# Keys and queries of six units turned by the vector engine instead of by matmul, in a delta-rule and mixer kernel

## The chip, the cores and the metric

One core of a Trainium2 chip runs the whole program. The metric is the time on the device in microseconds (us); the median of five runs is compared. The engines have short names in what follows: PE (matrix engine), DVE (vector), ACT (scalar), POOL (GpSimd), SP (the engine that here does nothing but issue DMAs).

## What is computed

```python
k_n = k / (np.linalg.norm(k, axis=-1, keepdims=True) + 1e-06)
for t in range(S):
    y[:, :, t] = einsum('bhd,bhde->bhe', q[:, :, t], state)
    v_old = einsum('bhde,bhd->bhe', state, k_n[:, :, t])
    state = state + beta_t * einsum('bhd,bhe->bhde', k_n[:, :, t], v[:, :, t] - v_old)
x = y with the heads side by side            # (4, 768, 384)
u = x + (xt @ U @ V).transpose(0, 2, 1)      # xt = x.transpose(0, 2, 1)
out = u + np.maximum(u @ w_ch1, 0.0) @ w_ch2
```

There are 4 batches, 8 heads, 768 tokens and 48 numbers per head. The mixer has rank 32 for the tokens and 1536 hidden channels. All data are 32-bit floats on the chip.

## The kernel before

The recurrence is cut into chunks of 64 tokens (`L`), 12 per batch. Half a batch, six chunks of all eight heads, is a *unit*; units 0 to 7 are numbered through the batches, so batch b has units 2b and 2b+1. For each unit the kernel prepares what does not depend on the state: the products of keys with keys (`pg`) and of queries with keys (`qk`), and the inverse of a triangular 64x64 matrix per chunk and head (`zt`).

- `load_keys(n)`, `load(n)`, `load_queries(n)` fetch k, v and q with tokens on partitions (`kn`, `vn`, `qn`), eight DMAs each. From unit 2 on all are issued by SP.
- `norms(n)` squares and sums the keys (the squares are put into a buffer that is not yet in use), and makes the factors `cp` and the scaled v.
- `grams(n)` has key pairs and query pairs of chunks. For each, `turn` brings two chunks onto head-dimension-on-partitions with four PE transposes (L529) and one ACT copy (L535) into `kq`; then `products` multiplies (L553) and the results go to `pg` (ACT) or, masked, to `qk` (DVE, L569).
- `blocks(n)` sends `pg` through DRAM into 96 rows of 32x32 blocks (L624, L635), scales them (`gs`, L652), inverts them on DVE with 31 pairs of operations (L668, L674), sends the result through DRAM again (L683) and reads it back in two layouts (`zt` L707, `zc` L710); two groups of small matmuls (`p_x` L722, `p_v` L736) fill the off-diagonal quarter. 32x32 blocks of `zc` are turned by DVE (`turned`, L695).
- `recur(b)` walks through the 12 chunks of a batch. Each chunk is a chain PE (`p_y`, L870), DVE (`rhs`, L900), PE (`p_s`, L907), ACT (`z`, L916), PE (L921, L929), DVE (`s`, L944).
- `front(b, i)` is the low-rank part of the mixer and the turning of its result; `wide(b, i)` has the two large matmuls, `p_f` (L1038) and `p_o` (L1058), in groups of three matmuls, and the stores of the result (L1029).

The weights arrive as two 32-bit words per number and are converted by DVE slice by slice (`load_weights`).

The order of all instructions is decided when the program is built. The parts above are Python generators; a planner in `run` keeps a modelled clock per engine, knows which named events (`need`, `emitted`) a part waits for, and emits at each step the part that could start earliest, with a preference for parts of a lower place number. Costs such as `step(sp=2.6)` are the planner's guesses. On the chip every engine then works through its own instructions strictly in that order, and waits at semaphores.

Buffers matter for the change: `kq`, `pg`, `qk` and `vn` have two copies, so those of unit n come free when `rec(n-2)`, the recurrence over unit n-2, is done; `qn` has one copy, used in turn by all units but unit 1.

Of the kernel before, what the change touches and what calls it, by code (L numbers as in the profile page):

```python
# [9 lines left out]
FP32 = mybir.dt.float32  # L10
# [17 lines left out]
def kernel(  # L28
# [154 lines left out]

    ident = const.tile([128, 128], FP32, name="ident")
    make_identity(nc, ident)
    beta_sb = unit.tile([B * H, S], FP32, name="beta_sb", tag="kq")
    nc.gpsimd.dma_start(out=beta_sb, in_=beta.rearrange("b h s -> (b h) s"))
    upper = conv.tile([128, 128], FP32, name="upper", tag="wide")
    nc.gpsimd.memset(upper, 1.0)
# [92 lines left out]
    def load_weights():  # L282

        slices = list(weight_slices())
        loaded = {}

        def start(i):  # L290
            dst, src, groups = slices[i]
            n = dst.shape[1]
            if i % 2:
                wide = stage[:, 0 : 2 * n].bitcast(I32).rearrange("p (n two) -> p n two", two=2)
            else:
                wide = conv.tile([128, n, 2], I32, name="wide")
# [12 lines left out]

        def load_all():  # L310
            for i in range(len(slices)):
                yield need(("weights", i - 2), *[("v", 0)] * (i == 1), *[("opened", 1)] * (i == 2))
                yield from start(i)

        begin(load_all(), 2.03)
        for i in range(len(slices)):
            dst = slices[i][0]
            yield need(("landed", i))

            if dst.shape[1] == WIDE and i >= 2 + KT * DFF // WIDE:  # L320
                yield need(("ksq", 2), *[("keys turned", 2, c) for c in range(UC // 2)])
# [38 lines left out]
            emitted(("weights", i), 0.2)  # L360
# [55 lines left out]
    def load(n):  # L416

        yield need(("rec", n - 2))
        kq = unit.tile([128, UC, 2, 2, 2 * L], FP32, name="kq")
        pg = unit.tile([128, UC, 2, 2, L], FP32, name="pg")  # L420
        qk = unit.tile([128, UC, 2, 2, L], FP32, name="qk")
        made[n] = kq, pg, qk
# [16 lines left out]
    def load_queries(n):  # L439
        yield need(("turned", n - 1), ("turned", 0))  # L440
        yield from fetch(n, "q", qn[:, :, :, 0:D], q, (0, 0))

    def norms(n):

# [6 lines left out]
        kn = keys[n][:, :, :, 0:D]  # L451
        if n > 2:

            ksq = made[n][0][:, UC // 2 :].rearrange("p c j i t -> p (c j i t)")
# [61 lines left out]
    def grams(n, place):  # L516


        yield need(("k", n), ("room", n), ("pg", 0 if n == 1 else -1))
        kn = keys[n]  # L520
        kq, pg, qk = made[n]

        def turn(ts, places):
# [8 lines left out]
                        ident,  # L532
                    )
            yield step(act=0.6, then=0.1, give=("one",))
            nc.scalar.copy(places, p_t)  # L535

        def products(c0, i):

# [8 lines left out]
            for c in range(2):  # L547
                for j in range(2):
                    for par, x in QUADS:
                        rows, cols = half(par, D), half(x)  # L550

                        to = half(1 - x) if par == 1 and i == 0 else cols
                        nc.tensor.matmul(  # L553
                            p_g[par][to, c, j],
                            kq[rows, c0 + c, j, 0, cols],
                            kq[rows, c0 + c, j, i, cols],
                            start=True,
                            stop=True,
                        )
# [14 lines left out]
                    )  # L574

        def key_pair(c0):
            if n > 2 and c0 + 2 > UC // 2:
                yield need(("ksq", n))
            yield from turn([(kn, c0), (kn, c0 + 1)], kq[:, c0 : c0 + 2, :, 0])
            emitted(("keys turned", n, c0 // 2))  # L580
            yield from products(c0, 0)
            emitted(("p", n, c0 // 2), 0.5)

        def query_pair(c0):
            yield need(("q", n), ("p", n, c0 // 2))
            yield from turn([(qt, c0), (qt, c0 + 1)], kq[:, c0 : c0 + 2, :, 1])
            yield from products(c0, 1)
            emitted(("g", n, c0 // 2), 0.5)

# [8 lines left out]
        yield need(*[("g", n, i) for i in range(UC // 2)])  # L598
        emitted(("grams", n))
        emitted(("turned", n))  # L600

    def blocks(n):

# [262 lines left out]
    def recur(b):  # L866
        def from_state(p, kq, cu, i, s_old, first):

            for j, par, x in heads:
                nc.tensor.matmul(  # L870
                    p[half(x ^ par), par, D * (2 * i + j) : D * (2 * i + j) + D],
                    kq[half(par, D), cu, j, i, half(x)],
                    s_old[half(par, D), x, j],
                    start=first and j == 0,
                    stop=(i == 0),
# [202 lines left out]
    order += [(recur(b), 5 + 0.01 * b) for b in range(1, B)]  # L1078
    for n in range(2, 2 * B):
        at = 0.01 * n + (3 if n < 4 else 5)  # L1080
        order += [(load_keys(n), at + 0.1), (load(n), at + 0.1), (load_queries(n), at + 0.5)]
        order += [(norms(n), at + 0.2), (grams(n, (at + 0.3, at + 0.4)), at + 0.3)]
        order.append((blocks(n), at + 0.6 if n == 2 else 5.6 + 0.01 * n))
    for b in range(B):
# [36 lines left out]
```

## Time and profile before

| | us |
|---|---|
| median of 5 runs (lowest, highest) | 677.28 (674.7, 681.59) |
| the profiled execution | 677.28 |
| its span from first to last instruction | 675.5 |
| PE busy in the span | 622.2 |
| DVE busy in the span | 318.1 |
| ACT busy in the span | 199.1 |

The span falls into these parts, by the start of the instructions on PE: units 0 and 1 are prepared up to about 59 us; `recur(0)` runs from 59 to 130; `front(0)` follows, and the mixer's first large matmul starts at 151.5. `recur(1)` runs from 196.5 to 290, `recur(2)` from 320.7 to 415 and `recur(3)` from 453 to 542, each with the mixer of the batch before it in its gaps. From 550 us on only the mixer is left. The granted clock of PE was 0.50 between 31 and 120 us and 1.00 from 151 us on.

In the tables of the profile that follow, a line names the source line, the engine, the operation and the tiles it writes and reads; `x8` is a count, and what stands in brackets is how long the engine had been idle before the instruction and what ended the wait. `SPq` is SP issuing DMAs: its duration is the issuing, not the transfer.

### The profile page before, as it was taken

To read this page: it belongs to the slowest core of one execution; us is meant where nothing else is said; L and a number is where in the kernel's file an instruction comes from. 1 tells how busy PE (TensorE), PEld (TensorE's weight loads), DVE (VectorE), ACT (ScalarE), POOL (GpSimd) and SP (SyncE) were. 2 spreads that over 40 slices of the span, in tenths; PEclk is the share of its full clock that TensorE was granted. 3 is DMA by queue.
4 is the path that set the end of the run, shared out by engine and by line. 5 is a ranking of instruction groups with operands and counts; after the bars stand their busy time and mean duration, and the time that the engine had idled before them with its cause. 6 is when DMAs were issued, how large, how long until landed. Compare 5 with 4: busy or idle time off the path is not lost.

```text
span 675.5 us, 19682 instructions
## 1 busy us (share of the span) xinstructions
PE 622.2 (92%) x8676; PEld 400.3 (59%) x8676; DVE 318.1 (47%) x795; ACT 199.1 (29%) x487; POOL 43.3 (6%) x84
## 2 busy tenths in 40 slices
PE   5649898759999999989999999999999999999997
PEld 4438787526555566546556655665555555555554
DVE  6667687579888124872942287368111011000000
ACT  2406455524221362144314422323221221110210
POOL 6451000100100000000000000000000000000000
PEclk9955555859999999999999999999999999999999
DMA  8586736552711332246033312410300000000000
GB/s 123 117 209 143 157 104 186 139 112 40 196 39 37 71 65 60 49 100 116 14 69 71 78 38 54 72 55 2 60 14 26 1 1 24 12 1 23 13 11 24
DMA packets 143892, 46.00 MB, mean 68 GB/s; under 512 B 136960, under 2 KB 140032, under 8 KB 143808
## 3 DMA queue, kind: packets, MB, share of 16 engines
q1 hardware_dynamic: 133952, 30.99, 22.6%
q0 software_dynamic: 3552, 12.88, 6.6%
q10 hardware_dynamic: 6304, 0.89, 0.8%
q8 instruction: 68, 1.11, 0.7%
q14 instruction: 16, 0.13, 0.1%
HBM read 33.62 MB, written 11.11 MB: 66 GB/s over the span
## 4 chain that ended last, share of the span: by engine, by line
PE 81%; DVE 7%; DMA 6%; ACT 2%; SPq 2%; issue 1%; ACTq 1%; DVEq 0%
PE p_o L1058 28%; PE p_f L1038 27%; PE p_y L870 4%; PE p_g L553 3%; PE p_t L529 3%; PE p_s L907 2%; PE p_s L921 2%; DMA scr<-xt 2%; PE p_y L929 2%; DVE xt L674 2%; DVE prod L668 2%; PE p_u L1005 1%; PE p_e L794 1%; DMA scr<-pg 1%; PE p_h L995 1%
## 5 line engine op out<-in xcount | busy, mean ns | idle before, releaser
L1038 PE MATMUL p_f<-ut,w_sb 128*128 128x384 f32 x576 | 202.3, 496 | 0.2 <-ACT h_f L1023 0.2
L1058 PE MATMUL p_o<-w_sb,h_f 128*128 128x384 f32 x576 | 201.1, 495 | 0.0
L1038 PEld LDWEIGHTS p_f<-ut,w_sb 128*128 128x128 f32 x576 | 104.5, 190 | 63.8 <-issue 0.6
L1058 PEld LDWEIGHTS p_o<-w_sb,h_f 128*128 128x128 f32 x576 | 104.8, 190 | 63.2
L1023 ACT ACTIVATE h_f<-p_f 128x384 f32<-128x384 f32 x96 | 47.1, 490 | 202.9 <-PE p_f L1038 202.8
L1028 DVE TENSOR_TENSOR x<-x,p_o 128x384 f32<-128x384 f32 x24 | 13.2, 553 | 131.5 <-PE p_o L1058 131.5
L674 DVE TENSOR_TENSOR xt<-xt,prod 96x112 f32<-96x112 f32 (+21 forms) x216 | 70.4, 326 | 7.4
L668 DVE TENSOR_TENSOR prod<-gs,xt 96x112 f32<-96x112 f32 (+21 forms) x216 | 70.0, 324 | 6.4 <-ACT xt L641 0.3
L553 PE MATMUL p_g<-kq 48*64 48x64 f32 x1536 | 39.8, 251 | 8.9 <-DVE qk L569 7.7
L944 DVE TENSOR_TENSOR s<-s,p_s 128x192 f32<-128x192 f32 x40 | 14.1, 352 | 69.9 <-PE p_s L921 66.3
L553 PEld LDWEIGHTS p_g<-kq 48*64 48x64 f32 x1536 | 33.5, 160 | 17.8 <-DVE qk L569 7.2
L951 ACT COPY x<-p_y 64x192 f32<-64x192 f32 x96 | 30.0, 313 | 39.2 <-PE p_y L929 34.0
L870 PEld LDWEIGHTS p_y<-s,kq 48*64 48x64 f32 x1408 | 29.0, 151 | 19.9 <-issue 11.2
L535 ACT COPY kq<-p_t 128x512 f32<-128x512 f32 x48 | 27.4, 587 | 40.2 <-PE p_t L529 40.0
L916 ACT COPY z<-p_s 128x192 f32<-128x192 f32 x48 | 15.3, 318 | 74.8 <-PE p_s L907 74.5
L870 PE MATMUL p_y<-s,kq 48*64 48x48 f32 x1408 | 34.8, 240 | 0.8 <-DVE s L944 0.6
L900 DVE TENSOR_TENSOR rhs<-vn,p_y 128x192 f32<-128x192 f32 x44 | 15.5, 352 | 41.5 <-PE p_y L870 41.0
L907 PEld LDWEIGHTS p_s<-rhs,zt 64*64 64x64 f32 x704 | 16.7, 149 | 22.4 <-issue 17.8
L921 PEld LDWEIGHTS p_s<-z,kn 64*64 64x64 f32 x704 | 16.1, 151 | 19.3 <-issue 16.5
L907 PE MATMUL p_s<-rhs,zt 64*64 64x48 f32 x704 | 22.4, 244 | 3.7 <-DVE qk L569 1.7
L637 POOL MEMSET xt<- 96x1056 f32 x6 | 5.9, 978 | 276.3 <-DMA scr<-xt 276.3
L529 PE MATMUL p_t<-ident,kn 128*128 128x128 f32 x84 | 16.3, 332 | 7.7 <-DMA kn<-in_k_dram 7.0
(122 smaller groups left out, 525.0 us busy)
## 6 DMA issues: line engine op xcount, KB each, us to landing
wide<-in_moe_w_ch_dram POOLq DMA_DIRECT2D x6, 768.0 KB, 5.7
stage<-in_moe_w_ch_dram POOLq DMA_DIRECT2D x6, 768.0 KB, 5.9
out_dram<-x SPq DMA_DIRECT2D x24, 192.0 KB, 1.9
kn<-in_k_dram SPq DMA_DIRECT2D x60, 72.0 KB, 2.8
qn<-in_q_dram SPq DMA_DIRECT2D x48, 72.0 KB, 3.2
vn<-in_v_dram SPq DMA_DIRECT2D x48, 72.0 KB, 2.5
gs<-scr SPq DMA_DIRECT2D x8, 384.0 KB, 3.7
scr<-xt SPq DMA_DIRECT2D x8, 384.0 KB, 4.3
```

The lines of the kernel that those rows point to most:

```text
L529: nc.tensor.transpose(p_t[:, x, j], t[:, c, 2 * j : 2 * j + 2].rearrange("p s d -> p (s d)"), ident,)
L535: nc.scalar.copy(places, p_t)
L553: nc.tensor.matmul(p_g[par][to, c, j], kq[rows, c0 + c, j, 0, cols], kq[rows, c0 + c, j, i, cols], start=True, stop=True,)
L668: nc.vector.tensor_tensor(out=prod, in0=gb[:, :, j : j + 1, j + 1 :].to_broadcast([NP, split, m, w]), in1=xb[:, :, 0:m, j : j + 1].to_broa ...
L674: nc.vector.tensor_tensor(out=xb[:, :, 0:m, j + 1 :], in0=xb[:, :, 0:m, j + 1 :], in1=prod, op=ALU.subtract,)
L870: nc.tensor.matmul(p[half(x ^ par), par, D * (2 * i + j) : D * (2 * i + j) + D], kq[half(par, D), cu, j, i, half(x)], s_old[half(par, D), ...
L907: nc.tensor.matmul(p_s[half(x), par, D * (2 + j) : D * (2 + j) + D], zt[half(x ^ par), cu, par, j], rhs[half(x ^ par), 2 * j + par], start ...
L921: nc.tensor.matmul(p_s[half(par), x, D * j : D * j + D], kn[half(x), cu, 2 * j + par], z[half(x), 2 * j + par], start=True, stop=True,)
L951: nc.scalar.copy(tokens_of(b, c, g), pair_of(p_y, 1)[half(g)])
L1023: nc.scalar.activation(hs[f], p_f, ACTF.Relu)
L1038: nc.tensor.matmul(p_f, w1_sb[:, t, f * 128 : (f + 1) * 128], ut[:, t], start=(t == 0), stop=(t == KT - 1),)
L1058: nc.tensor.matmul(p_os[c], hs[e][:, c * 128 : c * 128 + 128], w2_sb[:, e], start=(e == 0), stop=(e == FT - 1),)
```

## The change

For units 2 to 7 `turn` is no longer used. k and q are fetched from DRAM in a second layout, in which each 32x32 block of the wanted result stands transposed: 16 DMAs for each of the two, with 32 partitions and runs of 32 or 16 numbers. They go into one staging buffer, which is the old `qn`. One DVE instruction over 128 x 1536 then turns all blocks of a unit's keys, another one its queries. `kq` is split in two tiles, `kt` and `qt`, in the order that this transpose writes. The tokens-on-partitions copy of k is still fetched, for the norms and the state update; that of q is no longer. The squares for the norms now lie in `qt`. Units 0 and 1 are turned by PE as before.

```diff
+    def turn_all(n):
+        b, hf = divmod(n, 2)
+        stage = qn.rearrange("p c s d -> p (c s d)")
+        places = stage.rearrange("p (x j m d) -> p x j m d", x=2, j=2, d=BK)
+        yield need(("queries turned", n - 1))
+        for i, (name, src) in enumerate((("keys", k), ("queries", q))):
+            for par in range(2):
+                for half_d in range(2):
+                    rows = slice(L * par + BK * half_d, L * par + BK * half_d + BK)
+                    ds = slice(BK * half_d, min(D, BK * half_d + BK))
+                    for x in range(2):
+                        yield step(sp=1.2)
+                        for j in range(2):
+                            h = 4 * (x ^ par) + 2 * j + par
+                            nc.sync.dma_start(
+                                out=places[rows, x, j, :, 0 : ds.stop - ds.start],
+                                in_=src[b, h, hf * UC * L : (hf + 1) * UC * L, ds].rearrange(
+                                    "(m t) d -> t m d", t=BK
+                                ),
+                            )
+            emitted((name, n), 8.0)
+            yield need((name, n), ("room", n), *[("ksq", n)] * (i == 1))
+            yield step(dve=1.8)
+            nc.vector.transpose(made[n][0][i].rearrange("p x j c t -> p (x j c t)"), stage)
+            emitted((name + " turned", n), 0.1)
...
-        kq = unit.tile([128, UC, 2, 2, 2 * L], FP32, name="kq")
+        kq = [unit.tile([128, 2, 2, UC, L], FP32, name=x) for x in ("kt", "qt")]
...
         def key_pair(c0):
-            if n > 2 and c0 + 2 > UC // 2:
-                yield need(("ksq", n))
-            yield from turn([(kn, c0), (kn, c0 + 1)], kq[:, c0 : c0 + 2, :, 0])
-            emitted(("keys turned", n, c0 // 2))
+            if n < 2:
+                yield from turn([(kn, c0), (kn, c0 + 1)], kq[0][:, :, :, c0 : c0 + 2])
             yield from products(c0, 0)
...
         def query_pair(c0):
-            yield need(("q", n), ("p", n, c0 // 2))
-            yield from turn([(qt, c0), (qt, c0 + 1)], kq[:, c0 : c0 + 2, :, 1])
+            yield need(("q" if n < 2 else "queries turned", n), ("p", n, c0 // 2))
+            if n < 2:
+                yield from turn([(qt, c0), (qt, c0 + 1)], kq[1][:, :, :, c0 : c0 + 2])
             yield from products(c0, 1)
...
-        order += [(load_keys(n), at + 0.1), (load(n), at + 0.1), (load_queries(n), at + 0.5)]
+        order += [(load_keys(n), at + 0.1), (load(n), at + 0.1), (turn_all(n), at + 0.15)]
```

The operands of `products` and of `p_y` change only in the order of their dimensions; in each case a run of 64 numbers is read, as before. The planner sees other steps and so emits all engines' instructions after about 95 us in a somewhat different order.

More of the change, by code (lines that the diff above doesn't have):

```diff
@@ L185 @@
     make_identity(nc, ident)
-    beta_sb = unit.tile([B * H, S], FP32, name="beta_sb", tag="kq")
+    beta_sb = unit.tile([B * H, S], FP32, name="beta_sb", tag="kt")
     nc.gpsimd.dma_start(out=beta_sb, in_=beta.rearrange("b h s -> (b h) s"))
@@ L320, in load_weights @@
             if dst.shape[1] == WIDE and i >= 2 + KT * DFF // WIDE:
-                yield need(("ksq", 2), *[("keys turned", 2, c) for c in range(UC // 2)])
+                yield need(("ksq", 2), ("below", 1, 2), ("turned", 1))
             wide = loaded.pop(i)
@@ L437, in load @@
         yield from fetch(n, "v", vn, v, (2, 2) if n < 2 else (0, 0))
-    def load_queries(n):
-        yield need(("turned", n - 1), ("turned", 0))
-        yield from fetch(n, "q", qn[:, :, :, 0:D], q, (0, 0))
+    def turn_all(n):
[23 more added lines that the diff above has]
+            emitted((name + " turned", n), 0.1)
     def norms(n):
@@ L452, in norms @@
         if n > 2:
-            ksq = made[n][0][:, UC // 2 :].rearrange("p c j i t -> p (c j i t)")
+            ksq = made[n][0][1].rearrange("p x j c t -> p (x j c t)")
         else:
@@ L516, in grams @@
     def grams(n, place):
-        yield need(("k", n), ("room", n), ("pg", 0 if n == 1 else -1))
-        kn = keys[n]
+        yield need(("k" if n < 2 else "keys turned", n), ("room", n), ("pg", 0 if n == 1 else -1))
+        kn = keys.get(n)
         kq, pg, qk = made[n]
@@ L534, in turn @@
             yield step(act=0.6, then=0.1, give=("one",))
-            nc.scalar.copy(places, p_t)
+            nc.scalar.copy(
+                places.rearrange("p x j e t -> p e j x t"),
+                p_t.rearrange("p e j (x t) -> p e j x t", x=2),
+            )
         def products(c0, i):
@@ L554, in products @@
                             p_g[par][to, c, j],
-                            kq[rows, c0 + c, j, 0, cols],
-                            kq[rows, c0 + c, j, i, cols],
+                            kq[0][rows, x, j, c0 + c],
+                            kq[i][rows, x, j, c0 + c],
                             start=True,
@@ L600, in grams @@
         emitted(("turned", n))
+        if n == 0:
+            emitted(("queries turned", 1))
     def blocks(n):
@@ L871, in from_state @@
                     p[half(x ^ par), par, D * (2 * i + j) : D * (2 * i + j) + D],
-                    kq[half(par, D), cu, j, i, half(x)],
+                    kq[i][half(par, D), x, j, cu],
                     s_old[half(par, D), x, j],
```

## The prediction

> **What bounds the kernel now.** I read the page first, then busy time by stage, then the timeline of PE and of SP's queue around one handover between batches.
>
> ```profile
> PE 622.2 (92%) x8676; PEld 400.3 (59%) x8676; DVE 318.1 (47%) x795; ACT 199.1 (29%) x487; POOL 43.3 (6%) x84
> q1 hardware_dynamic: 133952, 30.99, 22.6%
> ...
> core 0: us, PE busy (x) PEld busy (x) DVE busy (x) ACT busy (x) POOL busy (x), PEclk, DMA share, GB/s
> 137.00:151.00 14.00, 8.11 (x56) 4.62 (x59) 11.02 (x32) 2.47 (x6) 0.00 (x0) 0.52 0.56 105
> 151.00:197.00 46.00, 44.09 (x511) 27.36 (x505) 40.11 (x87) 17.47 (x36) 2.76 (x4) 1.00 0.43 100
> 197.00:290.00 93.00, 92.05 (x1483) 56.28 (x1485) 52.46 (x145) 25.40 (x66) 0.98 (x1) 1.00 0.24 52
> 290.00:302.00 12.00, 9.94 (x134) 5.92 (x135) 8.88 (x26) 6.34 (x16) 0.00 (x0) 1.00 0.53 107
> 302.00:415.00 113.00, 112.98 (x1877) 69.91 (x1876) 60.48 (x165) 36.63 (x90) 1.95 (x2) 1.00 0.31 61
> ```
>
> The reader is to see that from 151 us PE never rests: 92.05 of 93 us, 112.98 of 113. The matmuls of the mixer (`p_f`, `p_o`) fill every gap of the recurrence, in an order fixed when the program is built. Work taken off PE after 151 us shortens the run, unless PE then waits for something else. Before 151 us PE is not the limit; 151 to 197 is shared with DVE (40.11 of 46 us), which converts the last weights and inverts unit 2.
>
> ```profile
> start us, us, engine line op out<-in xcount [idle before <-releaser]
> 141.70 1.65 PE L980 MATMUL p_tt<-tt,quarters 128*128 128x384 f32 x2 [7.70 <-DVE tt L977]
> 307.12 1.04 PE L529 MATMUL p_t<-ident,qn 128*128 128x128 f32 x8
> ...
> L535 ACT COPY kq<-p_t 128x512 f32<-128x512 f32 x48 | 27.4, 587 | 40.2 <-PE p_t L529 40.0
> L695 DVE STREAM_TRANSPOSE zn<-zc 128x384 f32<-128x384 f32 x6 | 3.4, 574 | 6.6 <-DMA zc<-scr 6.6
> L695 DVE STREAM_TRANSPOSE w_sb<-w_sb 128x256 f32<-128x256 f32 x6 | 2.4, 427 | 2.2 <-DMA w_sb<-scr 2.2
> ...
> 278.92 6.58 SPq L388 DMA_DIRECT2D qn<-in_q_dram  x8
> 289.69 0.34 SPq L1029 DMA_DIRECT2D out_dram<-x  x1
> 290.07 5.27 SPq L388 DMA_DIRECT2D vn<-in_v_dram  x8
> 295.44 6.05 SPq L388 DMA_DIRECT2D kn<-in_k_dram  x8
> 301.60 0.53 SPq L499 DMA_DIRECT2D scrc<-cts  x1
> 302.23 0.34 SPq L683 DMA_DIRECT2D scr<-xt  x1
> 304.32 0.32 SPq L505 DMA_DIRECT2D cp<-scrc  x1
> 305.26 2.02 SPq L707 DMA_DIRECT2D zt<-scr  x4
> 307.33 2.06 SPq L710 DMA_DIRECT2D zc<-scr  x4
> ```
>
> Two things. Eight PE transposes, which are two turns, take 1.04 us, so a turn of two chunks is 0.52 us of PE, much less than one would guess. And at the handover to batch 2 the queries of unit 5 are fetched at 278.92, ahead of the end of the recurrence at 289; then SP works through v and k, and only then writes unit 4's inverse (302.23) and reads it back (`zt`, `zc`). `recur(2)` begins at 320.7 on PE.
>
> **The change part by part.**
>
> *Removed.* 36 turns (units 2 to 7, three key and three query pairs each): 144 of 192 transposes on PE, 36 copies of 587 ns (21 us) on ACT. ACT is busy 29% and the copies are off the path: nothing for them. For the 24 turns of units 4 to 7: at 0.52 us 12.5 us; by the busy time of line L529 in 225 to 325 and 350 to 450 us 14.6 us (which counts overlapping ends). I take 13.5 us, all in the stretch where PE is full. The six of unit 3 (3.1 us) and of unit 2 (about 5 us, at half clock) lie before 197 us.
>
> Here a rule and the trace differ. The trace has 8 transposes in 1.04 us (130 ns each). The Trainium skill, VectorE: DVE Perf Modes, section The three transpose paths, prices a 128x128 transpose (bf16) at 390 ns on TensorE and 311 ns on VectorE, apart from saying that VectorE turns 32x32 blocks only. By the rule 24 turns would free 24 x 4 x 0.39 = 37 us of PE and the forecast would be some 24 us lower; by the row 13.5. The row decides: transposes in a row overlap.
>
> *Added on DVE.* 12 transposes of 128x1536. From the rows, 128x384 takes 574 ns and 128x256 427 ns, 1.15 ns for each further column: 574 + 1152 x 1.15 = 1.9 us; in all 23 us on an engine 47% busy. By the rule's 311 ns a block it would be 12 x 311 = 3.7 us. I take 1.9. The transpose of q also waits for the norm's reduction, which frees its place and ends long before q lands. After 197 us it is hidden by filler on PE, but for one: the keys of unit 5 stand between the two copies of `tt` in `front(1)`, where there is no mixer work left to hide it.
>
> *Added on SP.* Per unit 32 DMAs (16 for k, 16 for q, 48 or 24 KB each) take the place of 8 of q; k's old load stays, since the state update and the norms need it. Each new DMA has 32x12 = 384 runs, as many as an old one. The nearest rows are 5.27 us for 8 (0.66 each) from HBM and 2.06 us for 4 (0.52) with 32 partitions; in the crowded stretch before 110 us 8 took 6.75 (0.84). I take 0.6, ends 0.52 and 0.84: 9.6 us for 16, +14 us of SP per unit. The transfers: q1's mean packet is 0.226 x 675.5 x 16 / 133952 = 18 ns, so 6144 packets keep 16 engines 7 us, less than the issuing. For the 64-byte runs there is no row; half of 18 ns to twice it. Only at twice (14 us for 16 DMAs) would landing lag behind issuing, by about 4 us.
>
> *Moved.* One staging buffer serves k and q of every unit, and a transpose writes into `kt`/`qt` buffers that come free with `rec(n-2)`. So keys can be fetched ahead, but queries only after the keys are turned, right behind the handover. In SP's new order for units 4/5: v, k, 16 DMAs of q, scrc, 4 of `pg`, cp, then unit 4's inverse, unit 5's `gs`, `zt`, `zc`. Queued behind q5 is thus what `recur(2)` waits for.
>
> *By stretch.* 0 to 197: unit 2's keys are turned early, its grams leave PE about 3 us sooner, and `tt`, queued on DVE behind the `gs` product of unit 2, comes sooner by as much; q of unit 2 (16 DMAs behind v at 108.6, to 118) just clears SP. Against it stand two transposes in the DVE-bound part (3.8 us) and a second-layer weight slice that now lands after unit 2's `zn`, for which the first `p_o` wait about 3.5 us. I take -2.5, ends -6 and +4.
>
> Handover 1 (290): the mixer groups of batch 0 run out one chunk earlier, so the last chunk has only a product to hide its waits, +1.5; `tt` 1.9 later, of which the shorter PE work before it gives back half, +1. `p_f` of batch 1 begins near 300 instead of 301.5. Handover 2: `rec(3)` ends near 287; v 5.3, k 6, q 9.6, the small ones 3 us: inverse written at 311 instead of 302.23, landed 314; `gs`, `zt`, `zc` to 319, landed 321. PE's order puts ten groups of `p_f` (1.94 us each) and the q products ahead of `p_x`, so PE comes to `p_x` near 322.5: nothing lost, with 1.5 us to spare; at 0.84 per DMA 2 to 3 us. `recur(2)` starts some 8 us later than before, but six more mixer groups (11.7 us) are done by then. Handover 3: v, q, `pg` and a store that needs the last `p_o` of batch 1 stand before unit 6's inverse: about 22.5 us after `recur(2)`'s end, data there at 32.5, PE at `p_x` at 36.5. I add 1.5 for each of handovers 2 and 3 for waits that the order leaves. `front(3)` still has six groups to cover it: 1 us.
>
> Sum: -13.5 - 2.5 + 1.5 + 1 + 1.5 + 1.5 + 1 = -9.5 us. The profiled execution took 677.28 us (span 675.5 and 1.8 around it), and the median of the five runs is that same 677.28: 667.8, rounded to 668. The bound for "no change" is 0.5%, 3.4 us, about what a measurement of this kernel can tell.
>
> **The rivals.**
>
> *SP stalls the handover (slower).* If 16 queries and 16 others cost 0.84 to 1.1 us each, or land late, `zt` of handovers 2 and 3 comes 6 to 12 us after PE has reached `p_x`, and since PE's order is fixed nothing passes it. For: in the trace a wait of 7.70 us on PE (`tt`, 141.7) is followed by a clock of 0.52 over 137 to 151. The Trainium skill, TensorE: Matmul & The Clock Gate, section HAM oscillation, asks for no PE gap over about 3.4 us; the trace shows gaps of 2 us in 290 to 302 with the clock at 1.00. By the row my small gaps cost only themselves; by the rule the 3.5 us wait for a weight slice costs about 2 more at half clock, and the sum would be -7.5. A stall of 8 us costs 8 plus 7 of half clock (14 us at 0.52): one handover -9.5 + 15 = +5.5, 683; both, 698. It decides once SP is more than 9 us later than I reckon. Against: issues were 0.52 to 0.66 in this stretch, DMA share 0.31.
>
> *The gain is eaten (no change).* The chain inversion, SP, recurrence sets each stage, not PE; the freed 0.52 us pieces become waits in front of `p_s`, or DVE's transposes wait for q in front of `gs` and `zn`. For: before 197 us freed PE time already buys nearly nothing. Against: at the end of `recur(2)` nine groups of mixer were still waiting. About 677.
>
> *All is kept.* The start gains its 6 us and no handover waits: 13.5 + 6 = 19.5, 658.
>
> That it does not do what it says is excluded by the order of instructions: 12 stream transposes on DVE, 48 PE transposes left.
>
> **How the numbers follow.** Forecast (660 to 673.5) 0.50; all kept 0.10; no change 0.17; SP stall 0.23. Faster by over 0.5%: 0.60; within: 0.17; slower: 0.23. The range goes from 657 (all kept) to 686 (one stalled handover with its clock), which leaves out two stalled handovers and a little below; forecast's own range 660 to 673.5.
>
> **What would show it.** Right: PE busy within 1% of its windows from 300 us on, L529's group gone for units 2 to 7, transposes near 1.9 us, 16 staging DMAs in 8 to 11 us, `p_s` of `recur(2)` near 329, `p_tt` of `front(3)` 8 us later than 546 at most, `p_f` of batch 3 starting earlier than 579. Wrong: waits of PE on DMA `zt` or ACT `zt` over 5 us before `p_x` or `p_s`, a PEclk under 1.0 after 160 us, waits of DVE's transposes on DMA over 3 us each with PE idle beside them, or a start of `recur(1)` later than 200 us.

## The result, and the profile after

| us | median | lowest to highest, runs | ratio to before, 95% interval |
|---|---|---|---|
| kernel before | 678.85 | 674.7 to 682.78, 48 | 1 |
| changed kernel | 686.27 | 675.85 to 692.1, 27 | 1.0034 (1.001 to 1.0059) |

Medians here take all runs; a ratio leaves out each kernel's runs over 1.5% above its fastest, which are 15 of the changed kernel's 28 and none of the kernel before, so that the change costs 7.4 us by the medians and 0.3% by the ratio. No gain came: 668 was forecast. The kernel before keeps within 8 us, the changed one spreads over 16, and its profiled execution (688.91 us, span 687.2) is one of the long ones. What follows explains both the missing gain and the spread.

From the page of the changed kernel, PE's busy time, its clock in 40 slices, and the DMA queue that SP feeds:

```profile
PE 618.5 (90%) x8532; PEld 393.4 (57%) x8532; DVE 338.3 (49%) x807; ACT 180.9 (26%) x451; POOL 43.6 (6%) x84
PEclk9855555559979999988999999999999999999999
q1 hardware_dynamic: 191552, 34.53, 27.9%
```

144 matmul records are gone (8676 before, 8532 now), as the change says. Yet PE's busy time fell by only 3.7 us, since a part of the rest ran at a lower clock. The windows of the forecast, for the changed kernel (same columns as before):

```profile
core 0: us, PE busy (x) PEld busy (x) DVE busy (x) ACT busy (x) POOL busy (x), PEclk, DMA share, GB/s
137.00:151.00 14.00, 8.33 (x55) 4.11 (x55) 8.52 (x23) 1.43 (x3) 0.00 (x0) 0.61 0.58 98
151.00:197.00 46.00, 39.91 (x337) 24.61 (x341) 33.65 (x73) 12.54 (x28) 2.59 (x3) 0.91 0.43 83
197.00:290.00 93.00, 88.11 (x1427) 52.66 (x1419) 52.01 (x125) 25.09 (x61) 1.40 (x2) 0.96 0.38 71
290.00:302.00 12.00, 9.65 (x256) 6.57 (x256) 10.61 (x30) 2.52 (x7) 0.00 (x0) 0.94 0.41 69
302.00:415.00 113.00, 110.67 (x1640) 65.93 (x1632) 59.22 (x148) 33.99 (x85) 1.95 (x2) 0.96 0.40 71
```

Before, PEclk was 1.00 in all rows from 151 us on and PE was busy 44.09, 92.05 and 112.98 us in the 46, 93 and 113 us windows. Now every row is below 1.00, and PE rests 6 us in the 46 and 5 us in the 93.

A ledger sorts this. A span is PE's work at full speed, plus PE's idle time, plus half of the busy time at half clock. Idle and half-clock time are worked out from the trace (the gaps between PE's matmul records, and the clock's own records); work is what is left. It is an estimate: the same 8532 matmuls come out at 562.1 to 563.6 us of work in four profiles, and at 555.6 and 556.2 in two whose clock also stood at half for 10 us before 26 us.

| us | span | idle | lost at half clock | PE work | idle, lost after 151 us | `recur(1)` starts |
|---|---|---|---|---|---|---|
| before | 675.5 | 53.3 | 40.1 | 582.1 | 10.3, 0 | 196.5 |
| changed | 687.2 | 68.7 | 55.8 | 562.7 | 24.1, 12.6 | 208.3 |

The removed turns are there: PE's work fell by 19.4 us, 36 turns of 0.54. Idle time took back 15.4 and the clock 15.7; together that is the +11.7 of the two spans. Most of it arises after 151 us, where the forecast had PE full. `recur(1)` starts 11.8 us later. From there to the end the two profiles take 479.0 and 478.9 us: the time that the turns of units 4 to 7 free in this part is lost in it again. Before 151 us the clock stands at half for more than 100 us in both kernels.

Where the idle time arises shows in the timelines of the changed kernel around the start of `recur(1)`. First DVE:

```profile
start us, us, engine line op out<-in xcount [idle before <-releaser]
171.69 1.78 DVE L464 STREAM_TRANSPOSE kt<-qn 128x1536 f32<-128x1536 f32 x1
...
179.79 0.21 DVE L702 TENSOR_TENSOR xt<-xt,prod 96x31 f32<-96x31 f32 x1
...
187.86 1.77 DVE L464 STREAM_TRANSPOSE qt<-qn 128x1536 f32<-128x1536 f32 x1
197.99 0.58 DVE L723 STREAM_TRANSPOSE zn<-zc 128x384 f32<-128x384 f32 x1 [8.36 <-DMA zc<-scr]
198.49 0.92 DVE L356 SCALAR_TENSOR_TENSOR w_sb<-w_sb,power 128x768 f32<-128x768 f32 x1
...
204.53 0.96 DVE L356 SCALAR_TENSOR_TENSOR w_sb<-w_sb,power 128x768 f32<-128x768 f32 x1
```

then SP's queue:

```profile
173.50 9.04 SPq L455 DMA_DIRECT2D qn<-in_q_dram  x16
182.64 0.40 SPq L711 DMA_DIRECT2D scr<-xt  x1
183.14 2.94 SPq L652 DMA_DIRECT2D scr<-pg  x4
186.50 4.49 SPq L735 DMA_DIRECT2D zt<-scr  x4
191.03 5.15 SPq L738 DMA_DIRECT2D zc<-scr  x4
```

and PE:

```profile
189.77 1.16 PE L580 MATMUL p_g<-qt,kt 48*64 48x64 f32 x64 [0.35 <-DVE qt L464]
194.12 0.24 PE L750 MATMUL p_x<-zt,pg 32*32 32x32 f32 x2 [3.18 <-DMA zt<-scr]
196.12 1.50 PE L750 MATMUL p_x<-zt,pg 32*32 32x32 f32 x94 [1.76 <-DMA zt<-scr]
200.22 1.13 PE L580 MATMUL p_g<-qt,kt 48*64 48x64 f32 x32 [2.60 <-DVE qk L596]
201.28 1.50 PE L764 MATMUL p_v<-xz,zn 32*32 32x32 f32 x96
202.71 2.64 PE L1086 MATMUL p_o<-w_sb,h_f 128*128 128x384 f32 x4
205.59 2.82 PE L1086 MATMUL p_o<-w_sb,h_f 128*128 128x384 f32 x8 [0.24 <-issue]
```

Read from the top. The transpose of unit 3's keys stands in DVE's order in the middle of unit 2's inversion, at 171.69. The one staging buffer is free only then, so SP holds back unit 3's 16 query DMAs until 173.50, and they take 9 us. Unit 2's inverse is done at 180.00, but its way through DRAM (`scr<-xt`) begins only at 182.64. `zt` and `zc` then need 9.6 us of issuing. PE comes to `p_x` at 191 and waits 3.18, 1.76 and 2.60 us. Two groups of `p_o` (12 records, two for each matmul) stand behind. In this order they could not have filled the wait. The last step of converting their weights is at 198.49 for the first four records and at 204.53 for the fifth (both lines are in DVE's table), and both stand in DVE's order behind `zn`, where DVE itself waits 8.36 us for `zc`. So the late inverse stops two engines at once, and the second holds back what could have filled the first. The four records begin at 202.71, at half clock (2.64 us for the four), and the other eight at 205.59, right behind the end of the second conversion at 205.49.

The same place before, SP and then PE:

```profile
165.52 6.42 SPq L388 DMA_DIRECT2D qn<-in_q_dram  x8
174.03 0.32 SPq L683 DMA_DIRECT2D scr<-xt  x1
...
177.03 2.02 SPq L707 DMA_DIRECT2D zt<-scr  x4
179.10 3.41 SPq L710 DMA_DIRECT2D zc<-scr  x4
```

```profile
185.70 1.02 PE L722 MATMUL p_x<-zt,pg 32*32 32x32 f32 x96
186.65 2.20 PE L1058 MATMUL p_o<-w_sb,h_f 128*128 128x384 f32 x6
189.59 1.02 PE L736 MATMUL p_v<-xz,zn 32*32 32x32 f32 x96 [0.73 <-ACT xz L731]
```

There SP was free when the inverse was done, `zt` was there before PE asked for it, and `p_o` filled the time between `p_x` and `p_v`. `zn` came at 187.18, 10.8 us earlier than in the changed kernel.

The change also lets the second layer's weights wait for other events in the plan than before, a line that the diff ahead leaves out. Every kernel below that turns units 2 and 3 by PE has the old line back, so what this line costs was not tested apart.

### The profile page after: what moved, and what is told of

Same layout as the page of the kernel before. It is cut to its first block, busy times and chain, and to the rows that moved or that the text cites. A ratio compares the mean times of both kernels' runs of the same rounds, so it can differ in the third digit from the quotient of the medians.

```text
span 687.2 us, 19546 instructions
## 1 busy us (share of the span) xinstructions
PE 618.5 (90%) x8532; PEld 393.4 (57%) x8532; DVE 338.3 (49%) x807; ACT 180.9 (26%) x451; POOL 43.6 (6%) x84
## 4 chain that ended last, share of the span: by engine, by line
PE 75%; DVE 8%; SPq 7%; DMA 6%; issue 2%; ACT 1%; ACTq 1%; DVEq 0%
PE p_o L1086 27%; PE p_f L1066 26%; PE p_y L898 3%; PE p_g L580 3%; SPq L455 3%; PE p_s L935 2%; PE p_s L949 2%; PE p_u L1033 2%; DVE prod L696 2%; DVE xt L702 1%; PE p_y L957 1%; PE p_h L1023 1%; DMA scr<-xt 1%; PE p_e L822 1%; DMA scr<-pg 1%
## 5 line engine op out<-in xcount | busy, mean ns | idle before, releaser
L1086 PE MATMUL p_o<-w_sb,h_f 128*128 128x384 f32 x576 | 206.3, 502 | 0.6 <-DVE x L1056 0.4
L1066 PEld LDWEIGHTS p_f<-ut,w_sb 128*128 128x128 f32 x576 | 106.2, 192 | 67.5 <-issue 3.2
L944 ACT COPY z<-p_s 128x192 f32<-128x192 f32 x48 | 15.3, 318 | 93.3 <-PE p_s L935 93.0
L580 PE MATMUL p_g<-qt,kt 48*64 48x64 f32 x768 | 21.3, 262 | 11.4 <-DVE qk L596 10.4
L898 PEld LDWEIGHTS p_y<-s,kt 48*64 48x64 f32 x704 | 17.5, 153 | 21.0 <-issue 16.8
L580 PEld LDWEIGHTS p_g<-qt,kt 48*64 48x64 f32 x768 | 18.3, 169 | 17.6 <-issue 9.1
L898 PE MATMUL p_y<-s,kt 48*64 48x48 f32 x704 | 23.3, 247 | 2.9 <-issue 1.9
L898 PE MATMUL p_y<-s,qt 48*64 48x48 f32 x704 | 22.3, 240 | 1.8 <-issue 1.8
L957 PE MATMUL p_y<-z,qk 64*64 64x48 f32 x768 | 22.9, 240 | 1.0 <-ACT z L944 1.0
L949 PE MATMUL p_s<-z,kn 64*64 64x48 f32 x704 | 22.3, 248 | 1.6 <-ACT z L944 1.6
```

Of the source, the lines that this page charges most:

```text
L580: nc.tensor.matmul(p_g[par][to, c, j], kq[0][rows, x, j, c0 + c], kq[i][rows, x, j, c0 + c], start=True, stop=True,)
L898: nc.tensor.matmul(p[half(x ^ par), par, D * (2 * i + j) : D * (2 * i + j) + D], kq[i][half(par, D), x, j, cu], s_old[half(par, D), x, j], ...
L949: nc.tensor.matmul(p_s[half(par), x, D * j : D * j + D], kn[half(x), cu, 2 * j + par], z[half(x), 2 * j + par], start=True, stop=True,)
L957: nc.tensor.matmul(p_y[half(x ^ par), par, D * (2 + j) : D * (2 + j) + D], qk[half(x), cu, par, j], z[half(x), 2 * j + par], start=(c == 0 ...
L1066: nc.tensor.matmul(p_f, w1_sb[:, t, f * 128 : (f + 1) * 128], ut[:, t], start=(t == 0), stop=(t == KT - 1),)
L1086: nc.tensor.matmul(p_os[c], hs[e][:, c * 128 : c * 128 + 128], w2_sb[:, e], start=(e == 0), stop=(e == FT - 1),)
```

## The experiments

Three theories were put up after the result. Theory 1: SP's queue, with 32 staging DMAs per unit ahead of the inverse. Theory 2: with the turns gone PE has nothing to run at the stage starts, waits, and loses its clock. Theory 3: DVE's transposes stand in front of what PE waits for. A fourth, H, came from the timelines above: an order written for an earlier arrival blocks work that could run. H was put up for PE's order; that DVE's order takes part, as read above, shows in the traces.

**The changed kernel again.**

> The changed kernel once more, for a second profile and more times. Theory 1 (SP's queue): q's 16 staging DMAs stand in front of the previous unit's inverse on SP, so zt lands late, recur(1) starts near 208 us instead of 196.5 and recur(2) near 344 instead of 320.7, in every profile; the time is 676 to 692. Theory 2 (cold PE): the start of recur(1) moves by several us between profiles with where the half-clock windows fall, and a run with a clock of 0.91 has recur(1) near 200.

683.99 us (22 runs), ratio 0.9987 (0.9957 to 1.0018). The profiled execution was the one of 3139 us and tells nothing, so neither theory's forecast of `recur(1)` is answered by it. Of the 48 runs of the changed kernel, without one of 3139 us, 16 lie between 673 and 682 and 32 between 682 and 693. No kernel-before run passed 683.2.

**q of a unit fetched behind the inverse of the unit before.**

```diff
         for i, (name, src) in enumerate((("keys", k), ("queries", q))):
+            if i == 1:
+                yield need(("below", n - 1, 2))
```

> The changed kernel, but q of unit n is fetched only when the inverse of unit n-1 has been read back, so SP has the inverse first. Nothing is added or left out. Theory 1 (SP's queue): the read-back of unit 2 (zc) is issued near 182 instead of 191 to 196, recur(1) starts near 199 and recur(2) near 332, the time falls to 668 to 674. Theory 2 (cold PE and front without filler): recur(1) still starts after 205 and the time stays within 1% of the changed kernel's. Theory 3 (DVE: the transposes themselves delay the chain): little change too, within 0.7%.

685.66 us (22 runs), ratio 1.0008 (0.9976 to 1.0041). In its profile (676.31 us) `recur(1)` starts at 193.4 and `recur(2)` at 329.2, a little before the 199 and 332 that theory 1 gave. This profile is one of the short runs, though, with `p_f` at 143.3 instead of 151.9 for a reason that comes below, so the earlier starts are not the edit's alone. Idle after 151 us is still 21.8 us and 10.1 are lost at half clock. Moving the 16 query DMAs alone does not pay (668 to 674 was expected): theory 1 in this form falls.

**The staging DMAs issued by POOL.**

```diff
-                        yield step(sp=1.2)
+                        yield step(pool=1.3)
...
-                            nc.sync.dma_start(
+                            nc.gpsimd.dma_start(
```

> The changed kernel with all 192 staging DMAs issued by POOL instead of SP; same transfers, same transposes. Theory 1 (SP's queue): SP is as free as before the change, so recur(1) starts near 199 and the time is 666 to 673, about -1.5% to the changed kernel; if POOL's weight loads get stuck behind the staging DMAs, w2 comes late and the gain is half of that. Theory 2 (cold PE) and theory 3 (DVE): within 0.7% of the changed kernel. If it is the small transfers themselves (contention on the DMA engines), nothing changes either.

676.61 us (22 runs), ratio 0.9966 (0.9939 to 0.9993), 7.4 us under the 683.99 of the changed kernel, but short of the 666 to 673 of theory 1. So SP's issuing does cost, wherever it stands. The transfers are the same here, so they are not what costs these 7 us. The gain is at the long end: the shortest run is 1.8 us under the changed kernel's shortest, while 21 of the 22 runs end by 681.25, where the changed kernel goes to 692.94.

**The new layout alone, all turns by PE** (`if n < 2` becomes `if True` ahead of `turn`, and `load_queries` comes back).

> The kernel before with kq split into kt and qt in the new layout, and the squares of the norm in qt; PE turns all units as before, no staging DMAs, no DVE transposes of k and q. All theories: within 0.5% of the kernel before (674 to 681), recur(1) near 197. If the split and the strided ACT copy cost something themselves, ACT's 48 copies are longer than 587 ns and the time is over 681.

677.88 us (22 runs), ratio 0.9988 (0.9967 to 1.0009). The split of `kq` and its order cost nothing.

**The changed kernel with unread PE turns put back.**

```diff
+            p_t = ps_one([128, 2, 2, 2 * L], "p_t")
+            for x in range(2):
+                for j in range(2):
+                    nc.tensor.transpose(p_t[:, x, j], ident, ident)
```

> The changed kernel with TensorE's four transposes and their PSUM tile put back ahead of every pair's products in units 2 to 7; nothing reads them (48 turns, 192 transposes of a constant; no ScalarE copy of them). If TensorE's work was what these stages waited for, the freed 0.52 to 0.61 us per turn come back in full: 48 x 0.55 = +26 us at most, some +15 us on the changed kernel (about 700). If the freed time only became waiting at the stage starts, with a TensorE clock that drops to half in those waits (theory 2), the unread turns fill the same gaps as before: the time stays within 4 us of the changed kernel's 684 or goes below it, and the half-clock stretches after 151 us of the profile (17.1 + 10.2 + 3.4 + 6.8 us in the changed kernel, none in the kernel before) mostly go. If SP's order is what costs (theory 1), recur(1) still starts near 205 and the time is the changed kernel's plus part of the 15 us.

The text on record counts 48 turns; there are 36 (144 transposes, 19 us). 693.76 us (4 runs), ratio 1.0215 (1.0138 to 1.0292): 9 us over the changed kernel, about half of what was put back. In its profile 18.1 us are idle and 10.0 lost after 151 us, with half-clock stretches again at the start of `recur(1)` and at the handover. Theory 2's strong form, that the freed time is worth nothing, falls. The likely reason, not tested apart, is that these turns stand in the written order beside the products, behind the planned end of DVE's transposes: PE lacks filler at the place where it waits.

**Only units 4 to 7, or only units 2 and 3, by DVE** (`n < 2` becomes `not (n >= 4)` and `not (2 <= n < 4)`, with the old fetch of q for the others).

> Only units 4 to 7 are turned by VectorE; units 2 and 3 keep TensorE's transposes, and their q comes into SP's queue as in the kernel before. 32 of 48 turns are off TensorE. Both theories expect recur(1) at 196.5 us, as before. Theory 2 (gaps at the stage starts with a half clock): what is left of the loss is handovers 2 and 3, so a gain of at most 24 turns x 0.55 = 13 us in recur(1) and recur(2), less 4 to 8 us at the handovers: 668 to 673. Theory 1 (SP's queue): the same first stage, and the handovers pay SP's 9.6 us: 672 to 678. If the freed TensorE time in the recurrences is worth nothing at all: 677.

> Only units 2 and 3 are turned by VectorE; units 4 to 7 keep TensorE's transposes and the fetches of the kernel before. If the loss is at the start of recur(1) (12 us there in the changed kernel's profile, of which some 5 us of unit 3's turns come back inside recur(0)), recur(1) starts near 205 and the recurrence runs at the old pace after it: 680 to 686. If the loss is mainly at the later handovers, recur(1) is as late but the time is 673 to 678.

Here too the record says 32 of 48 turns where it is 24 of 36. The late units alone: 675.61 us (20 runs), ratio 0.9945 (0.9916 to 0.9974), `recur(1)` at 195.9 as before. The first two alone: 690.67 us (4 runs, over the 680 to 686 expected), ratio 1.017 (1.0102 to 1.0239), `recur(1)` at 208.0. Against the 678.52 of before that is -3 and +12, together +9, while the changed kernel stands at +5.4 and +7.4 in its two sets of runs. The loss is made by units 2 and 3, and the late units gain less than they free. Not all of the +12 arises before `recur(1)`: in the profile of the first two alone (699.2 us, the longest of the four runs) another 11.0 us are lost at half clock in the handover after it, from 302.7 to 326.6.

**Units 4 to 7 by DVE, their DMAs by POOL** (both edits).

> Units 4 to 7 turned by VectorE, with their 128 staging transfers issued by POOL's queue and not SP's; units 2 and 3 as before. A candidate for a version that beats both kernels. Handovers 2 and 3 have SP's queue free as in the kernel before, and recur(1) starts at 196.5: theory 1 expects 664 to 668 (24 turns x 0.55 = 13 us, nearly all kept), theory 2 expects no more than late_units_only gives, 668 to 675, since TensorE's gaps at the handovers do not depend on the queue.

671.14 us (663.0 to 677.39, 20 runs), ratio 0.9858 (0.9827 to 0.9889): faster than both kernels. Its ledger: PE work 568.7, which is 13.4 under before, and 11.6 idle with 6.3 lost after 151 us. PE at its first handover:

```profile
293.85 1.16 PE L584 MATMUL p_g<-kt 48*64 48x64 f32 x64 [1.21 <-DVE kt L468]
295.46 0.91 PE L1013 MATMUL p_tt<-tt,quarters 128*128 128x384 f32 x2 [0.45 <-DVE tt L1010]
...
298.72 0.55 PE L1038 MATMUL p_u<-ident,x 128*128 128x128 f32 x3 [0.65 <-DVE x L1034]
299.84 1.39 PE L1038 MATMUL p_u<-ident,x 128*128 128x128 f32 x6 [0.57 <-ACT ut L1041]
```

No wait here is over 1.3 us, and yet the clock falls at 300.0 for 6.8 us: the six records of `p_u` across that moment take 1.39 us, where the changed kernel ran six in 0.82 at full clock (317.18 us).

**Unit 2's products planned for a later arrival** (H).

```diff
-            yield step(sp=4.4, then=2.2)
+            yield step(sp=4.4, then=15.2 if n == 2 else 2.2)
```

> The changed kernel; in TensorE's written order the block products p_x and p_v of unit 2 stand behind nine more p_o matmuls and the third p_g group (the plan is told that zt arrives 13 us later); VectorE's zn moves with them. No work is added or taken away. In the changed kernel's profile TensorE stands 7.5 us idle at 191 to 200 us with those two products at the head of its queue while p_o matmuls behind them could run, and the clock is at half from 194.7 to 204.9. Theory H (the order written for an earlier arrival blocks TensorE, the clock then drops): the idle time before recur(1) falls from 8.9 to 3 us, the half-clock stretch at 195 us goes, recur(1) starts within 4 us of where it did, and the time falls by 5 to 10 us to 675 to 680. Theory 1 (SP's queue alone delays recur(1)): the same late start of recur(1) and no change of the time, 684.

> unit2_products_later again, on the same chip as the two others. Theory H expects a median of 674 to 678, 6 to 10 us under the changed kernel's 684 to 686. If its first six runs were luck: 682 to 686.

676.02 and 676.14 us (6 runs each). Both medians fall in a gap: six runs lie between 665 and 673 and six between 679 and 683, 8 to 10 us under the changed kernel at either end. The profiles (668.02 and 668.37 us) show 4.9 and 5.5 us idle from 151 us to `recur(1)`, where the changed kernel has 8.9. Half clock at this place got shorter, 6.8 and 3.4 us for 10.2, but did not go.

The edit moved more than PE's order. On DVE `zn` now stands behind the conversions (second profile):

```profile
177.89 0.92 DVE L356 SCALAR_TENSOR_TENSOR w_sb<-w_sb,power 128x768 f32<-128x768 f32 x1
...
184.10 0.96 DVE L356 SCALAR_TENSOR_TENSOR w_sb<-w_sb,power 128x768 f32<-128x768 f32 x1
...
190.03 0.57 DVE L723 STREAM_TRANSPOSE zn<-zc 128x384 f32<-128x384 f32 x1
```

DVE no longer waits at `zn`, and PE's first `p_o` behind the transposed queries run at 180.39, the fifth record at 185.16, right behind the second conversion. That the written order costs 8 to 10 us is shown. How much of it is PE's order and how much DVE's was not tested apart; with DVE's order as it was, no `p_o` was ready for PE before 199.4. `recur(1)` starts at 200.4 and 197.8, earlier than H said, and that has another cause, found by comparing these profiles with that of the changed kernel. Up to about 177 us they have the same order of instructions on every engine. The changed kernel, DVE and PE at `front(0)`:

```profile
138.22 1.22 DVE L680 TENSOR_TENSOR gs<-gs,cp 96x1024 f32<-96x1024 f32 x1 [6.47 <-DMA gs<-scr]
```

```profile
140.94 1.65 PE L1008 MATMUL p_tt<-tt,quarters 128*128 128x384 f32 x2 [4.14 <-DVE tt L1005]
...
151.90 4.05 PE L1066 MATMUL p_f<-ut,w_sb 128*128 128x384 f32 x6
```

and the second run of the reordered kernel:

```profile
131.92 1.22 DVE L680 TENSOR_TENSOR gs<-gs,cp 96x1024 f32<-96x1024 f32 x1 [1.86 <-DMA gs<-scr]
```

```profile
134.77 0.91 PE L1008 MATMUL p_tt<-tt,quarters 128*128 128x384 f32 x2
...
141.95 2.10 PE L1066 MATMUL p_f<-ut,w_sb 128*128 128x384 f32 x6
```

A DMA that lands 6.3 us sooner lets PE reach `p_tt` without a wait, the clock is full from 134 or 137 us to 185 (the two profiles), and the mixer starts 8 to 10 us sooner. With the wait of 4.14 us the clock falls again at 140.1 and stays at half to 157.2. Half of the 6.3 us is there when SP begins to write `pg` to DRAM (120.7 against 123.9 us); where that comes from was not followed further. The profiles of `q_behind_inverse` (676.31 us) and `staging_by_pool` (679.59 us), with `gs` at 133.4 and 133.0, are on the early side. The spread of the changed kernel fits this fork; for runs without a profile it is not shown. The kernel before and its control below wait long here (7.70 and 7.47 us in their profiles).

**The control: the kernel before with the same products later** (`then=12.2`).

> Control: the kernel before with unit 2's p_x placed fifteen p_o matmuls later in TensorE's order, nothing else. There TensorE waits 1.9 us in all from 151 us to recur(1) and its clock stays up, so theory H expects no gain: 677 to 682, with recur(1) some 5 to 10 us later. A gain of 5 us or more here would say that the place of these products was poor whatever the change did, and that unit2_products_later shows nothing about the change.

679.84 us (12 runs), ratio 0.9987 (0.9952 to 1.0022), as H said. The later place gains nothing by itself; it gained where `zt` and `zc` come late.

**PE's waits filled with unread transposes.**

```diff
+            for e in range(40 if b == 0 else 8):
+                nc.tensor.transpose(p_t[:, 128 * (e % 3) : 128 * (e % 3) + 128], ident, ident)
             nc.tensor.matmul(
                 p_t, quarters.rearrange("p i r -> p (i r)"), part, start=True, stop=True
             )
```

(and, in the same way, 6 ahead of `p_h` and 24 ahead of unit 2's `p_x`; the last only in the first of the two kernels.)

> The changed kernel with unread transposes of a constant put ahead of instructions at which TensorE waits, in the same PSUM tile, which the instruction behind then overwrites: 24 ahead of unit 2's p_x, 40 ahead of the second p_tt of front(0), 8 ahead of the second p_tt and 6 ahead of p_h of the other fronts. 133 transposes of 0.13 us are 17 us of added TensorE time if none of it fell into waits, and about 14 us of waits stand at these places in the changed kernel's profile (5.9 in front(0), 5 before p_x, 1 each at the p_tt and p_h). If the clock's drops are what costs (12.6 us lost at half clock after 151 us, 3 to 6 more before it), the half-clock stretches at 140, 195, 300 and 307 us shorten or go and the time falls by 4 to 12 us, to 673 to 680, in spite of the added work. If the drops do not matter or do not come from the waits: 684 to 692.

> late_units_by_pool (units 4 to 7 by VectorE, their transfers by POOL's queue) with the unread transposes of filled_waits at the fronts only: 40 ahead of front(0)'s second p_tt, 8 and 6 at the p_tt and p_h of the later fronts. Half clock in late_units_by_pool's profile: 139.6 to 156.7 and 300.0 to 306.8, 12 us of TensorE time together. If waits that are filled keep the clock up, it beats late_units_by_pool by 4 to 10 us: 661 to 667. If not, the added 11 us of transposes cost what does not fall into waits, some 3 us: 671 to 675.

`filled_waits`: 681.87 us (679.49 to 685.28, 12 runs), ratio 1.0036 (1.0015 to 1.0056). The time lost at half clock after 151 us falls from 12.6 to 4.6 us, and the spread from 19.5 to 6 us: with the waits filled the long runs are gone, and the shortest ones too (673.4 before). It gains 2 to 4 us, less than the 673 to 680 hoped for, since the transposes are work too. `late_by_pool_filled`: 675.27 us (12 runs), ratio 0.9937 (0.9913 to 0.9962), 4 us worse than without the filling, a miss. Two of its windows:

```profile
137.00:151.00 14.00, 12.17 (x172) 9.10 (x169) 10.78 (x33) 4.02 (x8) 0.00 (x0) 0.99 0.56 105
...
285.00:325.00 40.00, 36.40 (x546) 22.41 (x545) 31.93 (x79) 13.74 (x32) 20.37 (x33) 1.00 0.56 111
```

The clock held as intended (0.99 and 1.00; without filling 0.59 at 137 to 151). But PE's work rose by 14.0 us to 582.7, about what the clock gave back (15.3): the spans of the two profiles are 671.4 and 672.2. What parts the medians by 4 us, these two profiles do not show.

**Both remedies together** (POOL's queue, and `then=16.2`).

> The changed kernel with both remedies: the staging transfers issued by POOL's queue, and unit 2's p_x placed six p_o matmuls later in TensorE's order, with three more p_o ahead of p_v. TensorE's idle time before recur(1) in staging_by_pool was 10.6 us (4.4 before p_x, 3.1 before p_v), with a half-clock stretch of 17 us at 183. Theory H (order) with SP's queue as a second, separate part: the two add, so 684 - 8 (order) - 8 (queue), about 668 to 670, and recur(1) starts by 197. If both remedies take away the same loss: 676, as each alone.

678.03 us (12 runs), ratio 0.9994 (0.996 to 1.0028): they do not add. Its waits from 150 to 215 us (what waits, what it waits for, us in total, times, longest):

```profile
POOL qn L455 <- DVE kt L464: 14.0, 1, 14.0
...
PE p_o L1086 <- DVE w_sb L356: 7.5, 2, 5.5
```

The `p_o` that were brought forward now wait for weights that DVE has not yet converted, and POOL's queue stands behind DVE's transpose as SP's did. This is the second place where DVE's order decides what PE can run. How much of the loss the transposes on DVE make by themselves (theory 3) was not measured apart.

Shown, then: units 2 and 3 make the loss, taking the staging off SP's queue wins back 7 us of it, and a plan made for the later arrival 8 to 10; the two are not separate sums. How the loss divides between SP's queue, DVE's order, PE's order and the clock stays open.

## Why the prediction was wrong, step by step

*The turns removed: right.* 24 turns were to free 13.5 us; the ledger has 13.4 in `late_units_by_pool`, 11.3 in `late_units_only`, and 19.4 for all 36. The row (130 ns a transpose) gave the size, not the 390 ns that the forecast quotes beside it.

*The DVE transposes: right in size.* From the groups by line of the changed kernel:

```profile
L464 DVE STREAM_TRANSPOSE qt<-qn 128x1536 f32<-128x1536 f32 x6 | 10.7, 1775 | 0.2 <-issue 0.2
L464 DVE STREAM_TRANSPOSE kt<-qn 128x1536 f32<-128x1536 f32 x6 | 10.6, 1767 | 0.0
```

1.77 us against the 1.9 forecast.

*SP's issuing: right in size at the handovers.* SP at the handover to batch 2:

```profile
310.15 8.25 SPq L455 DMA_DIRECT2D qn<-in_q_dram  x16
...
324.19 0.30 SPq L711 DMA_DIRECT2D scr<-xt  x1
...
327.36 2.23 SPq L735 DMA_DIRECT2D zt<-scr  x4
```

16 DMAs took 8.25 us (9.6 forecast). The forecast's "0.52 to 0.66 in this stretch" was too kind to its own lines, where eight of `kn` took 6.05 and eight of `qn` 6.58 us (0.76 and 0.82 each).

*"0 to 197 ... I take -2.5": this step failed, and it is the largest error.* In the profiles `recur(1)` starts 11.8 us later, and units 2 and 3 alone cost +12, three times as far as the end of +4. The step looked at the queries of unit 2 ("just clears SP") and stopped. It did not carry the rule that it had itself stated, that queries can be fetched only after the keys are turned, on to unit 3: there the turn stands inside unit 2's inversion, and the 16 DMAs that it releases hold up the inverse's way through DRAM by 2.6 us (180.00 to 182.64), with slower issues behind them. SP's queue was followed at handovers 2 and 3 and not at the one place where DVE is nearly full too. The step did name the weight slice that comes behind `zn`, with a wait of 3.5 us. The place was right and the size was not: with `zn` 10.8 us later than before PE is idle for 7.5 us, `p_o` stops from 189.4 to 202.71, and the clock halves. The 16 DMAs are not the whole cause, since `q_behind_inverse`, which issues them later, is no faster. It also expected `tt` about 3 us sooner. In the profiles it comes 0.8 us sooner (140.94 against 141.70) or 5.6 to 6.9 us (136.10 to 134.77), and 10 us of the mixer's start hang on which.

*The handovers, +6.5 in sum: too small.* The late units were to bring -13.5 + 6.5 = -7. They brought -3 by SP and -7 by POOL, at the medians. SP's queue alone costs 4.5 us there, where 3 were put down for the waits at handovers 2 and 3, and the clock costs another few: 7.5 us are lost at half clock after 151 us in `late_units_only`, none before. In the profile of the whole change the part from `recur(1)` on got no shorter at all (479.0 and 478.9 us). The later start of `recur(2)` (344.3, forecast 329) is not in itself a loss: in this handover PE worked off 72 records of `p_f` where it had 36 before.

*The clock: the row was misread, and the rule is too wide.* The forecast took small gaps to cost only themselves, because the clock stood at 1.00 over 290 to 302 with 2 us of gaps. Those 2 us are a sum over 12 us; none of the 3.41 us steps at which the clock changes (see the last section) held more than 0.80 us of it. The Trainium skill, TensorE: Matmul & The Clock Gate, section HAM oscillation, puts the danger at gaps over about 3.4 us. Here a wait of 3.18 us and the start of the next halved the clock at 194.7, and the waits of 1.76 and 2.60 us fell into the 10.2 us that it lasted; waits of 0.65 and 0.57 us were enough at the handover of `late_units_by_pool`, for 6.8 us. One stage that kept its clock does not show that there was room.

*The rivals.* "SP stalls the handover" had the mechanism, a wait before `p_x` and then half clock, at a place the forecast did not look at. "The gain is eaten" had the size by the ratio; by the medians (+7.4 us) the 683 of one stalled handover is nearer. The forecast's own signs of failure came true: PEclk under 1.0 after 160 us, and `recur(1)` after 200.

## What to carry to other kernels

Follow every moved transfer at every stage where it occurs, above all the first, where other engines are full as well: here the late units gained 3 us and the first two lost 12. Work that is taken from an engine whose order is fixed pays only as far as what stands next in that order is ready; read the instruction that would come to the head of the queue, what it waits for, and what stands in front of that on the other engine. A change that wins in one part and loses in another is best cut in two: the four late units, with their transfers on an idle queue, gave 7.4 us (1.1% of the medians) where all six gave nothing.

## What the hardware showed that was not expected

In each of the fifteen profiles with records of the clock it changes only at whole steps of 3.41 us. Sorted by PE's idle time within one such step, from 125 to 655 us and at full clock: all 34 steps with more than 1.65 us were followed by half clock, 8 of the 25 with 1.0 to 1.65 us, and none of the 2111 with less. The step that ends at 300.0 in `late_units_by_pool` had 1.22 us, in two waits; one with 1.63 us, in `q_behind_inverse` at 487.3, kept its clock, and what decides between these is open. The way up is another: in the changed kernel the steps that begin at 58.2 and 65.0 us have no idle time at all, and the clock stayed at half until 136.7. The half-clock stretches after 125 us lasted 3.4 to 27.3 us.

Issuing got slower in a crowd: the four DMAs of `zt` took 4.49 us at 186 us and the four of `zc` 5.15, against 2.23 us for `zt` at the later handover and 2.02 before. It is not even: single DMAs of these eight took 0.47 to 2.32 us. The forecast's upper end, 0.84 us each, was too low for that place.
